# Who writes the waits: an agent attention and maxout FFN kernel whose semaphores are set by its own plan

## The chip, the cores and the metric

The kernel runs on one core of a Trainium2 chip. A core has five engines, each with its own instruction stream: PE (TensorE, matrix products), ACT (ScalarE), DVE (VectorE), POOL (GpSimd) and SP (SyncE, which here issues the transfers). They are kept in step by semaphores: an instruction may wait until a counter has reached a value, and may raise a counter when it is done. PE's products arrive in PSUM; everything else lies in SBUF. The metric is device time in microseconds (us); lower is better. The time before is 453.33 us, the median of three runs (451.63 to 454.15).

## The reference

Four batches of N = 12544 rows with C = 128 columns each, and 49 agents a batch. Agents first gather from keys and values, then each query gathers from the agents, and the result goes through a feed forward layer with three hidden branches of 768 columns:

```python
scale = 1.0 / np.sqrt(128)
a2k = softmax(scale * agents @ k.T)        # 49 x 12544
agent_v = a2k @ v                          # 49 x 128
q2a = softmax(scale * q @ agents.T)        # 12544 x 49
x = q2a @ agent_v                          # all batches: 50176 x 128
h = np.maximum(np.maximum(x @ w1, x @ w2), x @ w3)
out = h @ w_out
```

## The kernel before, in words

The kernel never forms x. For each batch it multiplies the 49 rows of agent values into the weights, w3 - w1, w2 - w1 and w1 @ w_out, and keeps the products in a tile G. A query's exponentials (49 values) times G then give the hidden layer directly. max(max(a, b), c) is computed as a plus two clipped differences, and the division by the softmax sum is done at the very end.

The work is cut into 49 groups s of 1024 rows (eight tiles of 128; the last group takes the last two tiles of each batch). For a group the steps are, with their names in the plan: `ql` loads the queries, `qc` casts them on POOL, `qt`/`qe` turn them on PE and copy them out on DVE (from s = 38 on a transposing transfer `qd` does it), `sc` and `ex` form scores and exponentials, `su` and `re` the reciprocal sums. Then for six blocks f of the hidden layer `u.s.f` (PE, line 558) and `a.s.f` (ACT, 571), `v.s.f` (PE, 558) and `x.s.f` (DVE, the max, 574); for f = 4 the clips are both on ACT (565 and 568) and `v` adds into the bank of `u`. Each hidden product is two matmuls on the two halves of the array's rows. `li` (582) and `p` (592) form the output in two halves o = 0, 1; `ov` (599) scales each half on DVE, and `st` (607) stores it.

Keys and values of batch 0 are worked first (steps `kl0`, `kc0`, `kt0`, `ke0`, `ks0`, `kx0`, `to0`, `vc0`, `kv0`); those of the next batches (`kl`, `kc`, `kt` as a transposing transfer, `ks`, `kx`, `kv`, `va`, `ea`, and at the end `fo`, `to`, `nr`, `gp`, `gv`) are hosted inside the query groups of the batch before.

The order of all steps, and the buffer that each new tile takes (the number after the slash), is written out by hand in the text `ORDER`: three two-bank PSUM buffers UV for hidden products, two PSUM banks OM for all else, thirteen load buffers LD and so on. Each engine executes its own steps in that order. What the text does not say is which instruction waits for which. In the kernel before this is found out by the framework that builds the program: a buffer is a tile of a pool with its number as tag, and every use of it is followed by the framework, which places waits and increments. Transfers share a small set of completion semaphores.

A step is a function of `Emit` that issues its instructions; `Plan.add` in `graph` states its engine, the steps that it follows (`after`), the tiles that it makes (`new`) and uses (`use`). The loop that runs them is:

```python
for name in order:
    o = plan.ops[plan.index[name]]
    for t in o["new"]:
        self.new(plan.tiles[t], t)
    o["fn"]()
```

Of the kernel before, what the change touches and what calls it, by code (L numbers as in the profile page):

```python
# [9 lines left out]
FP32 = mybir.dt.float32  # L10
BF16 = mybir.dt.bfloat16
# [16 lines left out]
PE, ACT, DVE, POOL, SP = range(5)  # L28
ROW, FULL, COL = range(3)
# [11 lines left out]
class Plan:  # L41
# [5 lines left out]
    def add(self, name, eng, fn, cost, mode=FULL, after=(), new=(), use=(), bank=None, serve=0.0):  # L47
        self.index[name] = len(self.ops)
        for cls, t in new:
# [4 lines left out]
                             new=[t for _, t in new], use=[t for _, t in new] + list(use), bank=bank, serve=serve))  # L54

    def places(self, order, given):
# [16 lines left out]
        return place  # L73

# [41 lines left out]
def graph(plan, em):  # L116
# [3 lines left out]
    add("prep", PE, em.prep, (0.3, 3.6))  # L120
# [21 lines left out]
    for g in range(SPARE):  # L142
        add(f"wm.{g}", PE, em.warm(g), (0.2225, 0.45), new=[("UV", f"warm.{g}")])
# [15 lines left out]
    add("rc0", DVE, em.recip_first, (0.85, 0.97), after=[f"to0.{g}" for g in range(last + 1)], new=[("KR", "kr0")], use=["acc"])  # L159
# [9 lines left out]
    add("el", ACT, em.evacuate_linear, (0.17, 0.31), after=["pl"], use=["pl"])  # L169
# [5 lines left out]
    for b in range(1, B):  # L175
        ch = chunks(b)
        for g, (t0, n) in enumerate(ch):
# [9 lines left out]
            add(f"ks{r}", PE, em.k_scores(b, g, n, m), mm(n, 49), after=[f"kt{r}"], new=[("OM", m)], use=[f"kT{r}"], bank=m)  # L187
# [72 lines left out]

class Emit:
    def __init__(self, nc, pools, io):
        self.nc, self.pools, self.io = nc, pools, io
        self.t, self.place = {}, {}
        nc_, const = nc, pools["const"]
        self.ident = const.tile([P, P], BF16, name="ident")
        make_identity(nc, self.ident)
        self.ones = const.tile([P, P], FP32, name="ones")
        nc.vector.memset(self.ones, 1.0)
        self.ones_bf = const.tile([P, P], BF16, name="ones_bf")  # L270
        nc.vector.memset(self.ones_bf, 1.0)
        self.avT = [const.tile([P, H], BF16, name=f"avT{i}") for i in range(2)]
        for t in self.avT:
            nc.vector.memset(t, 0.0)
        self.agT = const.tile([P, B, H], BF16, name="agT")
        nc.vector.memset(self.agT, 0.0)
        self.sel = const.tile([P, 2], BF16, name="sel")
        nc.vector.memset(self.sel, 0.0)
        nc.vector.memset(self.sel[:A, 0:1], 1.0)
        nc.vector.memset(self.sel[H:H + A, 1:2], 1.0)  # L280
        self.ag_st = const.tile([A, B, C], FP32, name="ag_st")
        nc.scalar.dma_start(self.ag_st, io["agents"].rearrange("b a c -> a b c"))
# [5 lines left out]
        nc.vector.memset(self.wall[:, C1O:], 0.0)  # L288
# [14 lines left out]
    def run(self, plan, order, given):  # L303
        self.place = plan.places(order, given)
        for name in order:
            o = plan.ops[plan.index[name]]
            for t in o["new"]:
                self.new(plan.tiles[t], t)
            o["fn"]()


    def prep(self):
        nc = self.nc
        nc.vector.tensor_copy(out=self.ag_bf, in_=self.ag_st)
        t = self.pools["psum"].tile([P, 512], FP32, tag="OM0", name="OM0").bitcast(BF16)
        for b in range(B):
            nc.tensor.transpose(t[:, b * H:b * H + A], self.ag_bf[:, b, :], self.ident[:A, :A])
        for b in range(B):
            nc.vector.tensor_copy(out=self.agT[:, b, :A], in_=t[:, b * H:b * H + A])
# [545 lines left out]
```

## Time and profile before

| what | value |
|---|---|
| median of three runs | 453.33 us (451.63 to 454.15) |
| profiled execution, first to last instruction (span) | 449.8 us |
| granted clock of PE | 0.996 |
| instructions | 13103 |
| PE, DVE, ACT busy | 94%, 90%, 88% of the span |
| POOL busy | 38% |
| DMA | 117.80 MB, mean 262 GB/s |

The profile gives of one execution the span alone; the time of a run is measured from outside and is some 3.5 us longer. In the profile's rows, PE is matmuls and PEld the loading of weights, which overlaps them; "TILE<-A,B" is the output and the inputs by the program's names; "[0.41 <-PE UV L558]" behind an instruction says that its engine was idle for 0.41 us before it, and that the product of line 558 into UV ended this. Instructions that only wait are not counted as busy.

### The profile page before, as it was taken

The numbers are of one execution on the slowest core, as the hardware profiler recorded it, in microseconds if no ns is written. First come the engines' busy times: TensorE is split into PE (matmuls) and PEld (weight loads), VectorE is DVE, ScalarE is ACT, GpSimd is POOL, SyncE is SP. The second block draws the span as 40 slices with busy tenths as digits, with TensorE's granted clock in tenths as the row PEclk, the third lists the DMA queues.
The fourth block names the chain that finished last, engine by engine and source line by source line (L and its number), as shares of the span: only waits on it lengthen the run. The fifth ranks groups of instructions, "written<-read, shape, count | busy, mean of one in ns | idle before, by whom it ended". The sixth has DMA issues, their size and how long they took to land.

```text
span 449.8 us, 13103 instructions
## 1 busy us (share of the span) xinstructions
PE 423.7 (94%) x5388; PEld 274.0 (61%) x5388; DVE 402.8 (90%) x512; ACT 395.1 (88%) x461; POOL 169.4 (38%) x176
## 2 busy tenths in 40 slices
PE   0778899999999999999999999999999999999996
PEld 0654466666665666666666666666666655565675
DVE  1335999999999999999999999999999999999986
ACT  1459999999988999999989999999889899999983
POOL 1641645455676372464363263453402110100000
PEclk9989999999999999999999999999999999999999
DMA  8999999999999998999969799498608685327142
GB/s 311 409 408 387 326 373 310 263 394 316 340 320 274 392 216 223 408 273 318 406 200 324 216 350 226 141 314 336 212 6 230 191 221 129 96 103 178 48 177 107
DMA packets 80150, 117.80 MB, mean 262 GB/s; under 512 B 53527, under 2 KB 56283, under 8 KB 80091
## 3 DMA queue, kind: packets, MB, share of 16 engines
q1 hardware_dynamic: 79888, 116.87, 83.6%
q8 instruction: 42, 0.69, 0.6%
q14 instruction: 17, 0.14, 0.1%
q10 hardware_dynamic: 203, 0.10, 0.1%
HBM read 78.74 MB, written 25.69 MB: 232 GB/s over the span
## 4 chain that ended last, share of the span: by engine, by line
PE 73%; DMA 12%; DVE 6%; POOL 2%; ACT 2%; SPq 2%; issue 2%; POOLq 0%; DVEq 0%
PE UV L558 29%; PE OM L592 27%; DMA LD<-in_k_dram 6%; PE OM L582 5%; DMA LD<-in_v_dram 4%; DVE R L574 4%; PE OM L523 3%; PE OM L533 3%; PE OM L376 2%; DMA out_dram<-OS 2%; PE OM L359 2%; DVE OS L599 1%; SPq L454 1%; ACT AS L571 1%; ACT VB L333 1%
## 5 line engine op out<-in xcount | busy, mean ns | idle before, releaser
L574 DVE TENSOR_TENSOR R<-UV,AS 128x1024 bf16<-128x1024 f32 x245 | 293.4, 1219 | 11.4 <-PE UV L558 5.3
L571 ACT ACTIVATE AS<-UV 128x1024 bf16<-128x1024 f32 x245 | 246.7, 1023 | 18.3 <-PE UV L558 11.7
L558 PE MATMUL UV<-EQ,G 49*128 49x512 bf16 (+1 forms) x1248 | 178.5, 368 | 2.1 <-DVE R L574 1.3
L592 PE MATMUL OM<-wo_bf,R 128*128 128x128 bf16 x2352 | 179.8, 219 | 0.0
L592 PEld LDWEIGHTS <-R 128*128 128x128 bf16 x2352 | 139.7, 98 | 39.5 <-issue 37.3
L558 PEld LDWEIGHTS <-G 49*128 49x128 bf16 x1248 | 58.7, 93 | 63.9 <-issue 23.8
L517 POOL CAST QB<-LD 128x1024 bf16<-128x1024 f32 x49 | 50.8, 1040 | 111.9 <-DMA LD<-in_q_dram 50.6
L599 DVE TENSOR_TENSOR OS<-OM,RC 128x512 f32<-128x512 f32 x98 | 67.3, 686 | 2.6 <-PE OM L592 1.4
L335 POOL CAST KB<-LD 128x1152 bf16<-128x1152 f32 (+2 forms) x45 | 49.7, 1116 | 40.6 <-DMA LD<-in_k_dram 35.9
L335 POOL CAST VB<-LD 128x1152 bf16<-128x1152 f32 (+1 forms) x33 | 37.3, 1137 | 40.4 <-DMA LD<-in_v_dram 24.3
L568 ACT ACTIVATE R<-UV 128x1024 bf16<-128x1024 f32 x49 | 50.1, 1022 | 2.5 <-PE UV L558 1.7
L565 ACT ACTIVATE UV<-UV 128x1024 f32<-128x1024 f32 x49 | 49.9, 1019 | 2.3 <-DVE R L574 1.2
L582 PE MATMUL OM<-G,EQ 128*128 128x256 bf16 x196 | 37.9, 275 | 0.0
L474 POOL TENSOR_TENSOR EA<-EA,EK 128x441 f32<-128x441 f32 x27 | 27.6, 1023 | 18.5 <-ACT EK L365 18.1
L539 ACT ACTIVATE EQ<-OM 128x512 bf16<-128x512 f32 x49 | 29.4, 601 | 1.0 <-PE OM L533 0.9
L527 DVE COPY QT<-OM 128x1024 bf16<-128x1024 bf16 x38 | 26.0, 684 | 1.1 <-PE OM L523 1.0
L347 DVE COPY KT<-UV 128x1152 bf16<-128x1152 bf16 (+1 forms) x12 | 8.2, 700 | 18.2 <-PE UV L342 18.2
L523 PE MATMUL OM<-ident,QB 128*128 128x128 bf16 x304 | 23.7, 222 | 0.6 <-POOL QB L517 0.6
L582 PEld LDWEIGHTS <-EQ 128*128 128x128 bf16 x196 | 12.3, 97 | 15.9 <-issue 15.2
L523 PEld LDWEIGHTS <-QB 128*128 128x128 bf16 x304 | 18.5, 99 | 4.3 <-issue 2.6
L359 PEld LDWEIGHTS <-KT 128*128 128x128 bf16 x392 | 14.3, 98 | 10.0 <-issue 5.5
L533 PE MATMUL OM<-QT,agT 128*64 128x512 bf16 (+1 forms) x104 | 20.2, 393 | 0.0
(67 smaller groups left out, 196.4 us busy)
## 6 DMA issues: line engine op xcount, KB each, us to landing
LD<-in_q_dram SPq DMA_DIRECT2D x48, 512.0 KB, 6.6
out_dram<-OS SPq DMA_DIRECT2D x48, 512.0 KB, 6.3
LD<-in_k_dram SPq DMA_DIRECT2D x40, 576.0 KB, 7.8
LD<-in_v_dram SPq DMA_DIRECT2D x40, 576.0 KB, 9.4
LD<-in_k_dram SPq DMA_DIRECT2D x3, 512.0 KB, 6.0
LD<-in_v_dram SPq DMA_DIRECT2D x3, 512.0 KB, 11.4
LD<-in_moe_w_dram SPq DMA_DIRECT2D x6, 192.0 KB, 8.4
KT<-KB SPq DMA_TRANSPOSE x33, 6.7
```

The source lines that it names most:

```text
L335: (self.nc.gpsimd if eng == POOL else self.nc.vector).tensor_copy(out=out, in_=src)
L517: return lambda: self.nc.gpsimd.tensor_copy(out=self.t[f"qb.{s}"], in_=self.t[f"q.{s}"][:, :GT, :])
L523: self.nc.tensor.transpose(t[:, j * P:(j + 1) * P], self.t[f"qb.{s}"][:, j, :], self.ident)
L533: self.nc.tensor.matmul(self.t[f"qs.{s}"][h * H:(h + 1) * H, jj * P:(jj + pairs) * P], self.agT[:, b, :], self.t[f"qT.{s}"][:, 2 * jj + h: ...
L558: self.nc.tensor.matmul(t[:, h, jj * P:(jj + pairs) * P], self.t[f"G{b}"][h * H:h * H + A, c + f * P:c + (f + 1) * P], self.t[f"e.{s}"][h ...
L565: return lambda: self.nc.scalar.activation(self.t[f"u.{s}.{f}"], self.t[f"u.{s}.{f}"], AF.Relu)
L568: return lambda: self.nc.scalar.activation(self.t[f"r.{s}.{f}"], self.t[f"u.{s}.{f}"], AF.Relu)
L571: return lambda: self.nc.scalar.activation(self.t[f"a.{s}.{f}"], self.t[f"u.{s}.{f}"], AF.Relu)
L574: return lambda: self.nc.vector.tensor_tensor(out=self.t[f"r.{s}.{f}"], in0=self.t[f"v.{s}.{f}"], in1=self.t[f"a.{s}.{f}"], op=ALU.max)
L582: self.nc.tensor.matmul(self.t[f"o.{s}.{o}"][:, i * 2 * C:(i + 1) * 2 * C], self.t[f"e.{s}"][:, jj * P:(jj + 1) * P], self.t[f"G{of[jj]}"] ...
L592: self.nc.tensor.matmul(self.t[f"o.{s}.{o}"][:, c:c + C], self.t[f"r.{s}.{f}"][:, h, jj * P:(jj + 1) * P], self.wo_bf[:, f, :], start=Fals ...
L599: self.nc.vector.tensor_tensor(out=self.t[f"os.{s}"][:, j:j + 4, :], in0=self.t[f"o.{s}.{o}"].rearrange("p (j c) -> p j c", c=C), in1=self ...
```

## The change

Order, buffers and arithmetic stay. The kernel no longer lets the framework find the waits. All buffers become fixed tiles, one for each place, and the new function `Plan.waits` walks the order once and works out for every step which earlier steps it has to wait for: those named in `after`, the makers of its tiles, the last users of a buffer that it takes over, and whoever else touched a PSUM bank. It keeps for each engine (and each destination of transfers) how far the others are known to have come, including what those had waited for themselves; what is already known is left out. Of steps of PE and of SP on their own engine nothing is waited for. `Emit.run` then issues the waits: all but the last as separate wait instructions in the engine's stream, the last one on the first instruction of the step. Only steps that somebody waits for raise a counter, with their last instruction; every transfer raises the counter of its destination buffer by 16. After the last step POOL waits for the final value of every counter. All of it stands in a critical section of the framework.

So that the plan knows everything, what was set up outside the order (identity, ones, agents) becomes steps of it; the preparation, the first reciprocal, the fold and the normalisation, whose instructions depend on one another, are split into one step for each, and a few steps name predecessors that they did not name before.

```diff
-    def add(self, name, eng, fn, cost, mode=FULL, after=(), new=(), use=(), bank=None, serve=0.0):
+    def add(self, name, eng, fn, cost, mode=FULL, after=(), new=(), use=(), bank=None, serve=0.0, dma=False):
         self.index[name] = len(self.ops)
         for cls, t in new:
             self.tiles[t] = cls
             self.maker[t] = name
         seq = [self.maker[t] for t in use if self.maker[t] not in after]
         self.ops.append(dict(name=name, eng=eng, fn=fn, pace=cost[0], lat=cost[1], mode=mode, after=list(after), seq=seq,
-                             new=[t for _, t in new], use=[t for _, t in new] + list(use), bank=bank, serve=serve))
+                             new=[t for _, t in new], use=[t for _, t in new] + list(use), bank=bank, serve=serve,
+                             dma=dma or eng == SP))
...
+    def waits(self, order, place):
+
+        known = {e: {} for e in range(5)}
+        snap, at, count = {}, {}, {}
+        users, slot_users, seen = {}, {}, {}
+        out, told = {}, set()
+        rank = {n: i for i, n in enumerate(order)}
+        for name in order:
+            o = self.ops[self.index[name]]
+            e = o["eng"]
+            need = set(o["after"])
+            for t in o["use"]:
+                cls = self.tiles[t]
+                key = (cls, place[t])
+                if t in o["new"]:
+                    slot_users[t] = users.get(key, {})
+                    users[key] = {}
+                m = self.maker[t]
+                if m != name and m not in need and (cls in PSUM or self.ops[self.index[m]]["eng"] == e):
+                    need.add(m)
+                elif t in o["new"] or m not in need:
+                    need.update(slot_users[t].values())
+                if cls in PSUM:
+                    need.update(x for k, x in users[key].items() if k != (e, False))
+            need.discard(name)
+            here = known[e]
+            todo = {}
+            for x in need:
+                p = self.ops[self.index[x]]
+                who, pos = at[x]
+                if who == e and (e == PE or e == SP):
+                    continue
+                if who not in todo or todo[who][0] < pos:
+                    todo[who] = (pos, x)
+            kept = []
+            for who, (pos, x) in sorted(todo.items(), key=lambda z: str(z[0])):
+                if here.get(who, -1) >= pos:
+                    continue
+                if any(w != who and snap[y].get(who, -1) >= pos for w, (_, y) in todo.items()):
+                    continue
+                kept.append(x)
+            for x in kept:
+                who, pos = at[x]
+                for w, v in list(snap[x].items()) + [(who, pos)]:
+                    if here.get(w, -1) < v:
+                        here[w] = v
+                told.add(x)
+            kept.sort(key=lambda x: rank[x])
+            out[name] = kept
+            who = e if not o["dma"] else (o["lane"] if "lane" in o else self.lane(o, place))
+            pos = count.get(who, 0)
+            count[who] = pos + 1
+            at[name] = (who, pos)
+            snap[name] = dict(here)
+            for t in o["use"]:
+                users[(self.tiles[t], place[t])][(e, o["dma"])] = name
+        return out, told, at
+
+    def lane(self, o, place):
+        t = o["new"][0] if o["new"] else o["use"][0] if o["use"] else None
+        return "AG" if t is None else f"{self.tiles[t]}{place[t]}"
...
-    add("prep", PE, em.prep, (0.3, 3.6))
+    add("id0", POOL, em.clear_ident, (0.3, 0.6))
+    add("id", POOL, em.make_ident, (0.3, 0.6), after=["id0"])
+    add("ones0", DVE, em.make_ones, (1.0, 1.1))
+    add("ones", DVE, em.make_sel, (0.15, 0.2), after=["ones0"])
+    add("agl", ACT, em.load_agents, (0.5, 5.0), dma=True)
+    add("agc", DVE, em.cast_agents, (0.42, 0.52), after=["agl"])
+    add("agt", PE, em.turn_agents, (0.2, 0.4), after=["agc", "id"], new=[("OM", "agt")])
+    add("prep", DVE, em.place_agents, (0.4, 0.5), after=["agt", "ones"], use=["agt"])
...
-    add("rc0", DVE, em.recip_first, (0.85, 0.97), after=[f"to0.{g}" for g in range(last + 1)], new=[("KR", "kr0")], use=["acc"])
+    add("rs0", DVE, em.reduce_first, (0.5, 0.6), after=[f"to0.{g}" for g in range(last + 1)], new=[("KR", "kr0")], use=["acc"])
+    add("rc0", DVE, em.recip_first, (0.35, 0.4), after=["rs0"], use=["kr0"])
...
-            add(f"ks{r}", PE, em.k_scores(b, g, n, m), mm(n, 49), after=[f"kt{r}"], new=[("OM", m)], use=[f"kT{r}"], bank=m)
+            add(f"ks{r}", PE, em.k_scores(b, g, n, m), mm(n, 49), after=[f"kt{r}", "prep"], new=[("OM", m)], use=[f"kT{r}"], bank=m)
...
-        add(f"fo{b}", POOL, em.fold(b), (1.25, 1.35), after=[f"ea{b}.{g - 1}"], new=[("ES", f"es{b}")], use=[f"ea{b}"])
+        for i in range(3):
+            add(f"fo{b}.{i}", POOL, em.fold(b, i), (0.33, 0.4), after=[f"fo{b}.{i - 1}" if i else f"ea{b}.{g - 1}"], use=[f"ea{b}"])
+        add(f"fo{b}", POOL, em.fold(b, 3), (0.25, 0.3), after=[f"fo{b}.2"], new=[("ES", f"es{b}")], use=[f"ea{b}"])
...
-        add(f"nr{b}", DVE, em.normalise(b, m), (0.5, 0.62), after=[f"to{b}", f"va{r}"], new=[("KR", f"kr{b}"), ("G", f"G{b}")],
-            use=[m, f"va{b}"], bank=m)
+        held = [f"gp{x}" for x in "abcd"] + ["gl"] if b == 2 else [f"gp{x}{b - 2}" for x in "acl"] if b > 2 else []
+        add(f"kr{b}", DVE, em.reciprocal_of(b, m), (0.25, 0.3), after=[f"to{b}"], new=[("KR", f"kr{b}")], use=[m], bank=m)
+        add(f"nr{b}", DVE, em.normalise(b, m), (0.25, 0.32), after=[f"kr{b}", f"va{r}"] + held, new=[("G", f"G{b}")],
+            use=[f"kr{b}", f"va{b}"])
...
-            add(f"gp{name}{b}", PE, em.product(b, c0, c1, f"gp{name}{b}"), mm(1, w), mode=COL, after=[f"nr{b}", "el"],
+            add(f"gp{name}{b}", PE, em.product(b, c0, c1, f"gp{name}{b}"), mm(1, w), mode=COL, after=[f"nr{b}", "el", "d31a", "d31b", "d32", "d21a", "d21b"],
...
+class Recorder:
+
+
+    def __init__(self, engine, made):
+        self.engine, self.made = engine, made
+
+    def __getattr__(self, name):
+        call = getattr(self.engine, name)
+
+        def record(*args, **named):
+            i = call(*args, **named)
+            self.made.append(i)
+            return i
+        return record
+
+
+class Engines:
+    def __init__(self, nc):
+        self.made = []
+        for n in ("tensor", "vector", "scalar", "gpsimd", "sync"):
+            setattr(self, n, Recorder(getattr(nc, n), self.made))
...
-    def new(self, cls, name):
-        shape, dt = SHAPE[cls]
-        tag = f"{cls}{self.place[name]}"
-        t = self.t[name] = self.pools["psum" if cls in ("UV", "OM") else "sbuf"].tile(shape, dt, tag=tag, name=tag)
-        return t
+        for cls, n in SLOTS.items():
+            shape, dt = SHAPE[cls]
+            for i in range(n):
+                self.slots[cls, i] = pools["psum" if cls in PSUM else "sbuf"].tile(shape, dt, name=f"{cls}{i}")
+
+    def run(self, plan, order, place, tc):
+
+        made = self.nc.made
+        for t, i in place.items():
+            self.t[t] = self.slots[plan.tiles[t], i]
+        waits, told, at = plan.waits(order, place)
+        sems, count, mark, final = {}, {}, {}, {}
+        for name in order:
+            o = plan.ops[plan.index[name]]
+            for x in waits[name][:-1]:
+                who, value = mark[x]
+                self.queues[o["eng"]].wait_ge(sems[who], value)
+            made.clear()
+            o["fn"]()
+            for x in waits[name][-1:]:
+                who, value = mark[x]
+                made[0].wait_op(sems[who], value, "sem-ge")
+            if o["dma"] or name in told:
+                who = at[name][0]
+                if who not in sems:
+                    sems[who] = tc.alloc_semaphore(f"s{who}")
+                for i in made if o["dma"] else made[-1:]:
+                    step = 16 if o["dma"] else 1
+                    i.then_inc(sems[who], step)
+                    count[who] = count.get(who, 0) + step
+                mark[name] = (who, count[who])
+                final.pop(who, None)
+                final[who] = count[who]
+        for who, value in final.items():
+            self.queues[POOL].wait_ge(sems[who], value)
...
-    with tc.manual_schedule():
-        em.run(plan, order, given)
+    place = plan.places(order, given)
+    with tc.tile_critical():
+        em.run(plan, order, place, tc)
```

More of the change, by code (lines that the diff above doesn't have):

```diff
@@ L168, in graph @@
     add("pl", PE, em.prep_linear, mm(NF, 128), after=["ew1", "cwo"], new=[("OM", "pl")])
-    add("el", ACT, em.evacuate_linear, (0.17, 0.31), after=["pl"], use=["pl"])
+    add("el", ACT, em.evacuate_linear, (0.17, 0.31), after=["pl", "ones"], use=["pl"])
     add("gl", PE, em.product(0, C1O, WC, "gl"), mm(1, 256), mode=COL, after=["nr0", "el"], new=[("OM", "gl")])
@@ L301, in half, with cast_agents, turn_agents, place_agents @@
         return t.bitcast(BF16)
[L303 to L315, printed above, removed]
+    def cast_agents(self):
+        self.nc.vector.tensor_copy(out=self.ag_bf, in_=self.ag_st)
+    def turn_agents(self):
+        t = self.half("agt")
         for b in range(B):
-            nc.tensor.transpose(t[:, b * H:b * H + A], self.ag_bf[:, b, :], self.ident[:A, :A])
+            self.nc.tensor.transpose(t[:, b * H:b * H + A], self.ag_bf[:, b, :], self.ident[:A, :A])
+    def place_agents(self):
         for b in range(B):
-            nc.vector.tensor_copy(out=self.agT[:, b, :A], in_=t[:, b * H:b * H + A])
+            self.nc.vector.tensor_copy(out=self.agT[:, b, :A], in_=self.half("agt")[:, b * H:b * H + A])
     def kv_load(self, which, b, t0, n):
```

66 lines of the change are left out of this document (36 added, 30 removed).

## The prediction

> **What bounds the kernel now.** I read the page first: the busy shares, the chain that ended last, then the groups.
>
> ```profile
> span 449.8 us, 13103 instructions
> PE 423.7 (94%) x5388; PEld 274.0 (61%) x5388; DVE 402.8 (90%) x512; ACT 395.1 (88%) x461; POOL 169.4 (38%) x176
> PE 73%; DMA 12%; DVE 6%; POOL 2%; ACT 2%; SPq 2%; issue 2%; POOLq 0%; DVEq 0%
> ...
> L574 DVE TENSOR_TENSOR R<-UV,AS 128x1024 bf16<-128x1024 f32 x245 | 293.4, 1219 | 11.4 <-PE UV L558 5.3
> L571 ACT ACTIVATE AS<-UV 128x1024 bf16<-128x1024 f32 x245 | 246.7, 1023 | 18.3 <-PE UV L558 11.7
> ```
>
> Three engines are near full and each hands to the next, so a share does not say which one decides; the chain is 73% on PE. A busy PE is not PE at its peak, so I looked at how often matmuls really start. This is PE's timeline: start, length, line, count.
>
> ```profile
> 285.10 0.38 PE L592 MATMUL OM<-wo_bf,R 128*128 128x128 bf16 x4
> 285.41 0.82 PE L558 MATMUL UV<-EQ,G 49*128 49x512 bf16 x6
> 286.17 0.39 PE L582 MATMUL OM<-G,EQ 128*128 128x256 bf16 x2
> 286.39 0.39 PE L592 MATMUL OM<-wo_bf,R 128*128 128x128 bf16 x4
> 286.62 0.61 PE L523 MATMUL OM<-ident,QB 128*128 128x128 bf16 x8
> 287.06 0.39 PE L592 MATMUL OM<-wo_bf,R 128*128 128x128 bf16 x4
> 287.38 0.89 PE L558 MATMUL UV<-EQ,G 49*128 49x512 bf16 x6
> 288.21 1.01 PE L592 MATMUL OM<-wo_bf,R 128*128 128x128 bf16 x15
> ```
>
> Eight L523 take 287.06 - 286.62 = 0.44 us, 55 ns each; two L582 take 0.22, 110 ns each; the four L592 at 286.39 take 0.23 to the next start, 57 ns each. Six L558 are three products (two halves of the array side by side): 0.76 and 0.83 us. Three products at 0.215 are 0.645, and about 0.1 us is left whenever PE turns between full and split matmuls: the four L592 at 285.10 take 0.31 up to L558, 0.22 of it matmuls. So PE does in a quiet stretch what these prices say:
>
> ```profile
> 260.00:300.00 40.00, 40.00 (x531) 26.37 (x529) 39.07 (x50) 38.31 (x45) 20.91 (x20) 1.00 0.88 240
> ...
> 60.00:430.00 370.00, 367.48 (x4602) 233.91 (x4600) 357.77 (x437) 347.02 (x401) 144.76 (x147) 1.00 0.85 253
> ```
>
> (stretch, length, then busy time and count of PE, PEld, DVE, ACT, POOL, the granted clock, DMA share, GB/s). Over 60 to 430 us PE's groups are:
>
> ```profile
> L592 PE MATMUL OM<-wo_bf,R 128*128 128x128 bf16 x2156 | 165.6, 219 | 0.0
> L558 PE MATMUL UV<-EQ,G 49*128 49x512 bf16 x1084 | 164.1, 381 | 1.8 <-DVE R L574 1.3
> L582 PE MATMUL OM<-G,EQ 128*128 128x256 bf16 x182 | 35.2, 275 | 0.0
> L523 PE MATMUL OM<-ident,QB 128*128 128x128 bf16 x272 | 20.8, 219 | 0.0
> ```
>
> 2156 x 56 ns + 542 x 215 + 182 x 108 + 272 x 56 = 121 + 117 + 20 + 15 = 273 us; the small groups (L533, L359, L376, L545, the products of G) add about 31, and some 540 turns at 0.094, counted in the same timeline, add 51. That is 355 of 370 us. So the steady stage is PE's own work to within about 14 us, and only those 14 can be had from quicker waits. The clock is 1.00, so none of it is the clock. DVE needs 39.07 and ACT 38.31 of 40: close behind, and it is their lateness that makes PE wait.
>
> The first 40 us have another bound, transfers (DMA share 0.97), and SP's DMA issues there stop behind earlier transfers:
>
> ```profile
> 0.00:40.00 40.00, 22.48 (x320) 16.99 (x320) 12.69 (x33) 18.66 (x27) 14.09 (x19) 0.96 0.97 379
> ```
>
> **The change part by part.** It moves no arithmetic. Removed are wait instructions and waits; added are some wait instructions, and the place of a wait on its instruction changes.
>
> (1) *Waits that sat on an instruction of their own.* Before, 5388 + 5388 + 512 + 461 + 176 instructions are counted as work, 11925 of 13103; with 246 DMA issues about 930 are left that only wait or signal. Their price shows where an engine starts straight behind a product. Start of the product on PE against start of its reader:
>
> ```profile
> 237.10 0.60 PE L558 MATMUL UV<-EQ,G 49*128 49x512 bf16 x4
> ...
> 233.47 0.60 PE L558 MATMUL UV<-EQ,G 49*128 49x512 bf16 x4
> ...
> 427.99 0.39 PE L558 MATMUL UV<-EQ,G 49*128 49x512 bf16 x2
> ```
> ```profile
> 237.60 1.23 DVE L574 TENSOR_TENSOR R<-UV,AS 128x1024 bf16<-128x1024 f32 x1 [0.41 <-PE UV L558]
> ...
> 428.42 2.39 DVE L574 TENSOR_TENSOR R<-UV,AS 128x1024 bf16<-128x1024 f32 x2 [0.23 <-PE UV L558]
> ```
> ```profile
> 233.90 1.02 ACT L571 ACTIVATE AS<-UV 128x1024 bf16<-128x1024 f32 x1 [0.63 <-PE UV L558]
> ```
>
> At 237.10 the reader comes 0.50 us behind, at 233.47 and 427.99 0.43. DVE's max has two makers (PE and ACT), ACT's first relu one; the same max comes at either distance, so it is not the engine, and I take 65 ns as the price of a wait that ends on an instruction of its own, and the change puts the latest wait on the working instruction. It counts only where the reader is already waiting:
>
> ```profile
> ACT AS L571 <- PE UV L558: 11.7, 38, 0.8
> ...
> DVE R L574 <- PE UV L558: 5.3, 17, 0.6
> ...
> PE UV L558 <- DVE R L574: 1.3, 3, 0.8
> ```
>
> (total us, times, longest). 55 such waits at 65 ns are 3.6 us of reader time, but PE loses only where its bank is then late. Of some 96 places where PE starts right behind a releaser, 43 have a releaser that was itself late by such an instruction: 43 x 65 ns = 2.8, and about half of it is made up again before PE needs it. I take -2.5 (1.5 direct, the rest because each delay also makes later ones); ends: 0, and -14, all of PE's waiting; -5 is as far as I call plausible.
>
> (2) *Where PE's wait sits.* Before, a hidden product's wait for its bank stands on the matmul and its weights are loaded ahead. After, the wait is put on the first instruction of the step, and if that becomes the weight load, the load starts only when the bank is free:
>
> ```profile
> L558 PEld LDWEIGHTS <-G 49*128 49x128 bf16 x1248 | 58.7, 93 | 63.9 <-issue 23.8
> ```
>
> In the places where load and matmul begin together already, the reader came 0.43 instead of 0.42 behind, so the real price is about 14 ns: the matmul follows into the part of the array that is loaded. With some 92 waits that bind and 60 close to it, 150 x 14 ns = 2.1 at most; I take +1.0. If instead each costs the whole 93 ns it is 150 x 93 = +14, of which about +11 stays, since some fall into idle turns.
>
> The Trainium skill ("TensorE: Matmul & The Clock Gate", Step-by-step: what each phase is for) says that PE's queue reorders only weight loads, ahead of matmuls in flight; by that rule a load that carries a wait can no longer run ahead, and its section LDWEIGHTS (loading the stationary operand) would price it, as an estimate, at 128/1.2 = 107 ns, +16 us here. The trace has 93 ns for the same load, and no row of before shows a load held by a bank.
>
> (3) *Wait instructions on PE.* 130 to 150 steps of PE keep two waits (K scores: transfer and slot; values: ACT and POOL; turns: POOL and slot), so PE gets about as many new instructions. Behind each stand the products of the next tiles, and DVE and ACT wait for those. Most run under PE's queue; some 5 bind, 5 x 65 ns = +0.3 (0 to 140 x 65 ns = 9).
>
> (4) *Semaphores per destination.* Shared ones make a DMA issue wait for an unrelated transfer, in the start above all: loads go out about 1.5 us apart there.
>
> ```profile
> 11.35 0.33 SPq L391 DMA_DIRECT2D LD<-in_moe_w_dram  x1
> 12.85 0.33 SPq L325 DMA_DIRECT2D LD<-in_v_dram  x1
> ```
>
> But the DMA share is 0.97, so an earlier issue only queues: -0.3 (0 to -1). Cover gone, i.e. engines not full, each such wait would be worth about a microsecond.
>
> (5) *Entry and end.* The whole plan runs in a critical section with an own final wait of POOL for every counter. Nothing in the trace shows such a section; the nearest rows are the opening up to the first load and the last:
>
> ```profile
> 0.74 0.87 SPq L325 DMA_DIRECT2D LD<-in_k_dram  x2
> ```
>
> The setup, one barrier among it, takes 0.74: I take +0.2 at entry (0 to 0.74) and +0.3 at the end (0 to 0.74).
>
> (6) *The last store.* Before, the first of st.48's four transfers leaves when half the output is scaled:
>
> ```profile
> 445.65 1.79 SPq L607 DMA_DIRECT2D out_dram<-OS  x4
> ```
> ```profile
> 444.93 1.36 DVE L599 TENSOR_TENSOR OS<-OM,RC 128x512 f32<-128x512 f32 x2 [0.59 <-PE OM L592]
> ```
>
> After, the step waits for both halves: 444.93 + 1.36 = 446.29 instead of 445.65, and the four issues stand one behind the other: +0.6.
>
> The split preparation, fold and normalisation (0 each) issue the same instructions in the same order; POOL, with 20.91 busy of 40, hides the fold, and DVE's stall for the normalisation was there.
>
> Sum: -2.5 + 1.0 + 0.3 - 0.3 + 0.2 + 0.3 + 0.6 = -0.4 us on a span of 449.8. Median before 453.33, 3.5 us above that span (451.63 to 454.15); the parts outside the span do not change, so 453.33 - 0.4 = 452.9 us.
>
> **The rivals.** *Quicker handovers propagate.* PE, DVE and ACT form one loop, and a delay in each comes back as a later bank. For it: three engines at 38 to 40 of 40 us and 14 us of PE's waiting. Against: in the quiet stretch hardly anything is waited for. If half the waiting goes: -7 + 1.9 = -5, 448 us.
>
> *Weight loads are held by their waits* (ends on the other side). Place: the first matmul of each hidden product; price 93 ns; it decides once more than 30 of the 150 are exposed (30 x 93 = 2.8, more than part 1 gives). For it: the wait goes on the first instruction of a step. Against: the 14 ns seen where both start together. +11 - 2.5 + 0.4 = +9, 462 us.
>
> *The critical section costs a real barrier at both ends* and waits on PE bind more often: +1.5 at entry and end, +2 on PE: 456 us.
>
> *It prunes what never bound*: the waits that decide are the ones kept, everything of part 1 is 0: 453.33 + 2.1 = 455.4, no change that can be told.
>
> **How the numbers follow.** About 0.5%, 2.3 us, is what a measurement of this kernel can tell from no change. Forecast as summed: 0.38, its own range 450.5 to 455; propagation 0.34, spread over 446 to 451; loads held 0.11; section 0.09; pruned for nothing 0.08. Faster takes propagation and a little of the forecast's lower end: 0.38. Slower takes loads, section and a little of the upper end: 0.21. Same: 0.41. The range leaves out the worst of the loads case and the far end of propagation: 446 to 458.5.
>
> **What would show it.** Part 1: DVE's max starts 0.43 instead of 0.50 behind its product, and the idle time before L574 and L571 falls from 11.4 and 18.3. Part 2: L558's weight loads start together with their matmuls, and the distance to the next product tells 14 or 93 ns. Part 3: PE's turns to L359, L376 and L523 lengthen. Part 4: the loads at 11 to 20 us leave closer together without landing earlier. Part 6: the last store leaves at the end of the second L599. Wrong would be a PE whose waits beyond 60 us shrink by half (faster than forecast), or turns that grow above 0.1 us (slower).

## The result, and the profile after

The changed kernel takes 455.97 us (median of 12 runs, 453.88 to 458.6) against 452.33 (median of 12, 451.18 to 454.71) of the kernel before: ratio 1.0077, 95% interval 1.0054 to 1.010. It is slower by 0.8%, some 3.5 us. The forecast was 452.9 and no change; the range, 446 to 458.5, holds the time, but slower had only 0.21.

All instructions now carry one line, L347, because one recording function issues them; read them by their tiles. The page after, in the order of the page before:

```profile
span 454.3 us, 12617 instructions
PE 424.4 (93%) x5388; PEld 264.3 (58%) x5388; DVE 402.6 (89%) x512; ACT 395.2 (87%) x461; POOL 169.8 (37%) x176
PE 72%; DMA 14%; SPq 4%; ACT 3%; DVE 3%; POOL 2%; issue 1%; DVEq 0%
...
L347 DVE TENSOR_TENSOR R<-UV,AS 128x1024 bf16<-128x1024 f32 x245 | 292.8, 1218 | 9.4 <-PE UV L347 6.0
L347 ACT ACTIVATE AS<-UV 128x1024 bf16<-128x1024 f32 x245 | 246.8, 1023 | 20.2 <-PE UV L347 14.6
```

486 instructions are gone, and the work of each engine is the same. What is new is in the chain: SP's queue has 4% of it, 2% before. So I looked at where the 4.5 us of span arise, first by the scalings of the output (each 1024 rows end with one). Tile OS on DVE in two windows, 55 to 67 and 440 to 456 us; the times are those of the first and of the last start. Before:

```profile
L599 DVE TENSOR_TENSOR OS<-OM,RC x3: 680/692/694, 55.1 to 63.1; 128x512 f32<-128x512 f32 x3
...
L599 DVE TENSOR_TENSOR OS<-OM,RC x4: 681/688/692, 440.7 to 445.6; 128x512 f32<-128x512 f32 x4
```

After:

```profile
L347 DVE TENSOR_TENSOR OS<-OM,RC x2: 680/686/691, 60.1 to 64.2; 128x512 f32<-128x512 f32 x2
...
L347 DVE TENSOR_TENSOR OS<-OM,RC x5: 636/679/691, 439.4 to 449.1; 128x512 f32<-128x512 f32 x5
```

The first scaling comes 60.1 - 55.1 = 5.0 us late, the last 449.1 - 445.6 = 3.5. The loss is there before the first output; over the 48 groups behind it the changed kernel wins 1.5 us back. The rest of the span is the end: from the last scaling's start to the last instruction it is 454.3 - 449.1 = 5.2 us instead of 449.8 - 445.6 = 4.2. Together 5.0 - 1.5 + 1.0 = 4.5, the difference of the spans.

Now the start. Stretches of 3 us (length, PE, PEld, DVE, ACT, POOL, granted clock, DMA share, GB/s), before:

```profile
36.00:39.00 3.00, 2.17 (x21) 1.03 (x20) 0.66 (x2) 3.00 (x6) 0.00 (x0) 1.00 1.07 385
39.00:42.00 3.00, 2.50 (x36) 1.39 (x37) 2.11 (x7) 2.51 (x4) 0.00 (x0) 1.00 1.03 387
45.00:48.00 3.00, 2.00 (x19) 0.87 (x16) 2.92 (x3) 2.57 (x5) 2.79 (x3) 1.00 1.00 397
```

After:

```profile
36.00:39.00 3.00, 2.15 (x32) 1.14 (x30) 1.07 (x3) 3.00 (x6) 0.00 (x0) 1.00 0.43 159
39.00:42.00 3.00, 1.86 (x26) 0.73 (x22) 1.54 (x6) 1.52 (x3) 0.00 (x0) 1.00 0.67 192
45.00:48.00 3.00, 1.80 (x12) 0.88 (x10) 0.97 (x3) 1.99 (x3) 1.04 (x1) 0.50 1.01 362
```

From 36 to 42 us the transfers, which bound this stage, move less than half as much (159 and 192 GB/s instead of 385 and 387). Later PE's clock is at half. SP's timeline and its waits say why the transfers stop. After:

```profile
25.49 14.47 SPq L347 DMA_DIRECT2D LD<-in_moe_w_dram  x5
40.07 0.37 SPq L347 DMA_DIRECT2D LD<-in_q_dram  x1
40.48 0.43 SPq L347 DMA_DIRECT2D LD<-in_k_dram  x1
40.96 0.43 SPq L347 DMA_DIRECT2D LD<-in_moe_w_out_dram  x1
```
```profile
SPq L347 <- DMA LD<-in_moe_w_dram: 9.6, 1, 9.6
```

Before:

```profile
28.85 5.30 SPq L391 DMA_DIRECT2D LD<-in_moe_w_dram  x5
35.31 0.33 SPq L513 DMA_DIRECT2D LD<-in_q_dram  x1
36.72 0.33 SPq L325 DMA_DIRECT2D LD<-in_k_dram  x1
38.21 0.39 SPq L389 DMA_DIRECT2D LD<-in_moe_w_out_dram  x1
```

Five weight loads go out in 5.3 us before and in 14.5 after, with one wait of 9.6 us for a weight load. The three hidden weights are loaded in two halves each into one buffer (`lw1a` and `lw1b`, and so on). `Plan.waits` sees that `lw1b` uses the tile that `lw1a` made, on the same engine, and takes `lw1a` as needed; and since a transfer is on the list of its destination and not of SP, the rule that SP does not wait for itself does not spare it. So the second half waits until the first has landed, behind all that SP had put into the queue earlier, and everything behind it on SP waits too: the other two second halves, queries, keys of the next batch, w_out. The two halves write different columns; the wait protects nothing but the count, since both raise one counter.

### The profile page after: what moved, and what is told of

It reads as the page before. It is cut to its first block, busy times and chain, and to the rows that moved or that the text cites. A ratio compares the mean times of both kernels' runs of the same rounds, so it can differ in the third digit from the quotient of the medians.

```text
span 454.3 us, 12617 instructions
## 1 busy us (share of the span) xinstructions
PE 424.4 (93%) x5388; PEld 264.3 (58%) x5388; DVE 402.6 (89%) x512; ACT 395.2 (87%) x461; POOL 169.8 (37%) x176
## 4 chain that ended last, share of the span: by engine, by line
PE 72%; DMA 14%; SPq 4%; ACT 3%; DVE 3%; POOL 2%; issue 1%; DVEq 0%
PE OM L347 43%; PE UV L347 29%; DMA LD<-in_v_dram 6%; SPq L347 4%; DMA LD<-in_q_dram 3%; DMA KT<-KB 2%; DMA out_dram<-OS 2%; DMA LD<-in_moe_w_out_dram 2%; DVE R L347 2%; ACT AS L347 1%; ACT VB L347 1%; DVE OS L347 1%; POOL QB L347 1%; POOL KB L347 0%; POOL EA L347 0%
## 5 line engine op out<-in xcount | busy, mean ns | idle before, releaser
L347 DVE TENSOR_TENSOR R<-UV,AS 128x1024 bf16<-128x1024 f32 x245 | 292.8, 1218 | 9.4 <-PE UV L347 6.0
L347 ACT ACTIVATE AS<-UV 128x1024 bf16<-128x1024 f32 x245 | 246.8, 1023 | 20.2 <-PE UV L347 14.6
L347 PE MATMUL OM<-wo_bf,R 128*128 128x128 bf16 x2352 | 179.8, 219 | 0.0
L347 PE MATMUL UV<-EQ,G 49*128 49x512 bf16 (+1 forms) x1248 | 178.9, 372 | 0.6
L347 PEld LDWEIGHTS OM<-wo_bf,R 128*128 128x128 bf16 x2352 | 139.7, 98 | 39.6 <-issue 37.5
L347 POOL CAST QB<-LD 128x1024 bf16<-128x1024 f32 x49 | 50.9, 1042 | 109.3 <-DMA LD<-in_q_dram 60.6
L347 PEld LDWEIGHTS UV<-EQ,G 49*128 49x128 bf16 x1248 | 49.5, 93 | 71.4 <-ACT AS L347 16.9
L347 DVE TENSOR_TENSOR OS<-OM,RC 128x512 f32<-128x512 f32 x98 | 67.3, 687 | 4.5 <-PE OM L347 2.0
L347 POOL CAST KB<-LD 128x1152 bf16<-128x1152 f32 (+2 forms) x45 | 49.8, 1118 | 41.1 <-DMA LD<-in_k_dram 40.0
L347 POOL CAST VB<-LD 128x1152 bf16<-128x1152 f32 (+1 forms) x33 | 37.4, 1139 | 45.7 <-PE OM L347 29.5
L347 ACT ACTIVATE UV<-UV 128x1024 f32<-128x1024 f32 x49 | 49.9, 1019 | 3.9 <-PE UV L347 3.6
L347 ACT ACTIVATE R<-UV 128x1024 bf16<-128x1024 f32 x49 | 50.1, 1022 | 1.9 <-PE UV L347 1.5
L347 PE MATMUL OM<-G,EQ 128*128 128x256 bf16 x196 | 38.0, 275 | 0.0
L347 POOL TENSOR_TENSOR EA<-EA,EK 128x441 f32<-128x441 f32 x27 | 27.7, 1026 | 19.5 <-ACT EK L347 19.1
L347 ACT ACTIVATE EQ<-OM 128x512 bf16<-128x512 f32 x49 | 29.5, 601 | 1.3 <-PE OM L347 1.2
L347 DVE COPY QT<-OM 128x1024 bf16<-128x1024 bf16 x38 | 26.0, 684 | 3.3 <-PE OM L347 3.3
L347 PE MATMUL OM<-ident,QB 128*128 128x128 bf16 x304 | 24.5, 227 | 1.8 <-POOL QB L347 1.2
L347 DVE COPY KT<-UV 128x1152 bf16<-128x1152 bf16 (+1 forms) x12 | 8.2, 698 | 17.8 <-PE UV L347 17.8
L347 PEld LDWEIGHTS OM<-ident,QB 128*128 128x128 bf16 x304 | 19.1, 101 | 5.9 <-issue 2.7
L347 PEld LDWEIGHTS OM<-G,EQ 128*128 128x128 bf16 x196 | 12.1, 97 | 15.8 <-issue 7.8
L347 PE MATMUL OM<-QT,agT 128*64 128x512 bf16 (+1 forms) x104 | 20.6, 403 | 0.0
L347 ACT ACTIVATE EK<-OM 128x441 bf16<-128x441 f32 (+1 forms) x33 | 17.8, 539 | 1.5 <-PE OM L347 1.0
```

Of the source, the lines that this page charges most:

```text
L347: i = call(*args, **named)
```

## The experiments

**The wait alone, taken out and put in.** In the changed kernel each second half gets a counter of its own and no longer waits for the first:

```diff
         add(f"l{w}b", SP, em.w_load(w, DFF // 2, DFF), use=[w], **dma(196))
+        plan.ops[-1]["lane"] = f"{w}b"
...
                 m = self.maker[t]
-                if m != name and m not in need and (...):
+                if "lane" in o:
+                    need.update(slot_users[t].values())
+                elif m != name and m not in need and (...):
```

> The changed kernel, but the second half of each hidden weight no longer waits for the first half's transfer to land; each second half raises a counter of its own. Theory (the loss is that wait: SP stops, everything behind it on SP comes late): the DMA share between 36 and 45 us is back at about 1.0 (0.43 and 0.67 in the changed kernel), PE's granted clock stays at 1.0 after 45 us, the first group's output ends near 60 us instead of 64.9, and the time is 451 to 452 us, a little under the kernel before. Rival one (the start is late by its split preparation and its clock): the first output stays beyond 63.5 us and the time at 455 to 456. Rival two (the loss lies in the steady stage, where PE's waits sit on weight loads): the time stays above 454 too, and the lag grows group by group.

Measured: 452.04 us, ratio to the kernel before 0.9994 (0.9975 to 1.0012). Scalings, weight loads and one stretch of this kernel:

```profile
L350 DVE TENSOR_TENSOR OS<-OM,RC x3: 681/691/692, 55.0 to 63.0; 128x512 f32<-128x512 f32 x3
```
```profile
25.74 4.51 SPq L350 DMA_DIRECT2D LD<-in_moe_w_dram  x5
```
```profile
36.00:39.00 3.00, 2.28 (x23) 1.04 (x20) 0.60 (x1) 3.00 (x7) 0.00 (x0) 1.00 1.06 383
```

The loads go out in 4.5 us, the share is 1.06, the first scaling is at 55.0: the loss at the first output is gone with this one wait. The time is just at the upper end of the expected 451 to 452. This kernel's last scaling starts at 444.9 us. Against it the changed kernel is 60.1 - 55.0 = 5.1 us late at the first scaling and 449.1 - 444.9 = 4.2 at the last, so 0.9 of the 1.5 us above is, by these two traces, lateness that is made up on the way, and only 0.6 is won by the kernel with free halves too.

Then the kernel before, with nothing but that wait; its framework sets it when the halves overlap by one column:

```diff
-        add(f"l{w}b", SP, em.w_load(w, DFF // 2, DFF), use=[w], **dma(196))
+        add(f"l{w}b", SP, em.w_load(w, DFF // 2 - 1, DFF), use=[w], **dma(196))
```

> The kernel before with that wait alone: the second half of each hidden weight is loaded from one column earlier, so that the two halves overlap by a column (same values) and the framework makes the second wait for the first. Theory: 4 to 5 us slower than before, 456 to 457.5 us, with a hole in the DMA share after 36 us and a granted clock under 1.0 after 45 us. Rivals: within 1 us of the kernel before.

Measured: 457.65 us, ratio 1.0114 (1.0074 to 1.0154), a little above the expected 456 to 457.5. These are four runs that lie far apart, 454.78 to 459.96, and the profiled one is the fastest of them. The same hole appears in it:

```profile
28.64 11.10 SPq L391 DMA_DIRECT2D LD<-in_moe_w_dram  x5
```
```profile
36.00:39.00 3.00, 2.18 (x21) 1.04 (x21) 0.67 (x2) 3.00 (x6) 0.00 (x0) 1.00 0.43 161
39.00:42.00 3.00, 1.44 (x28) 0.83 (x28) 0.97 (x2) 1.83 (x2) 0.00 (x0) 1.00 0.69 208
...
L599 DVE TENSOR_TENSOR OS<-OM,RC x3: 682/691/691, 58.2 to 66.2; 128x512 f32<-128x512 f32 x3
```

The wait stands 6.9 us here instead of 9.6, the granted clock falls to 0.60 from 45 to 48 us, and the first scaling is 58.2 - 55.1 = 3.1 us late instead of 5.0.

Taken out of the one kernel and put into the other, the wait moves the time by -0.8% and +1.1%. That shows the cause from both sides; rivals one (the split preparation) and two (the steady stage) fall.

**Is the clock a part of it?** PE's clock of 0.5 after 45 us could have been the larger half of the damage. Idle matmuls were put into PE's holes in the changed kernel, first into one, then into all three:

```diff
     def warm(self, g):
-        return lambda: self.nc.tensor.matmul(self.t[f"warm.{g}"][:, 0, :], ...)
+        def fn():
+            for _ in range(10 if g == SPARE - 1 else 1):
+                self.nc.tensor.matmul(self.t[f"warm.{g}"][:, 0, :], ...)
+        return fn
...
- gvd cwo qt.1/0
+ gvd cwo wm.8/0 qt.1/0
...
- u.0.4/2 pl/1
+ u.0.4/2 wm.9/1 pl/1
```

(wm.8 and wm.9, eight matmuls each, are in the second run only.)

> The changed kernel, its weight halves still waiting, and ten idle matmuls instead of one in the hole before the product of the second weight halves (from 40.8 us on), so that PE does not fall idle there. It tells the clock's part of the loss from the late data's. If PE's clock of 0.5 from 45 to 54 us comes from that hole and costs what the first output lost beyond the late transfers (5.0 - 3.8 = 1.2 us): the clock stays at 1.0, the first output ends near 63.7, the time is about 1 us lower, 455. If the late data are all of it: the time stays at 456 whatever the clock.

> The changed kernel, its weight halves still waiting, with idle matmuls in all three holes that PE has between 41 and 50 us: ten ahead of the product of the second weight halves, eight each ahead of the turn of the second query group and of the product of w1 with w_out. In the run before, with the first hole alone filled, the clock fell later, from 51 to 58 us, instead. If the clock's fall is part of the loss: with all holes filled the clock stays at 1.0, the first output ends 1 us or more earlier than 64.9 and the time is 455 us or less. If the late data are all of it: the first output at 64 to 65 and the time at 456, although the clock stays.

Measured: 456.27 us, ratio 1.0093 (1.0068 to 1.0119), and 455.99, ratio 1.0060 (1.0038 to 1.0083), where the changed kernel has 1.0077. With one hole filled the clock fell later (to 0.57 and 0.50 from 51 to 57 us), with all three it stayed up. Stretches and scalings of the second:

```profile
45.00:48.00 3.00, 2.63 (x16) 1.07 (x15) 1.87 (x4) 2.56 (x3) 0.34 (x1) 1.00 1.07 378
48.00:51.00 3.00, 3.00 (x23) 1.41 (x22) 1.82 (x2) 1.01 (x1) 2.48 (x3) 1.00 1.04 412
```
```profile
L349 DVE TENSOR_TENSOR OS<-OM,RC x2: 680/686/691, 59.8 to 63.9; 128x512 f32<-128x512 f32 x2
```

The clock is 1.00 instead of 0.50, and the first scaling still starts at 59.8 instead of 60.1. So the clock alone does not make the loss. How much of it is the clock's stays open, for two reasons. The ratios 1.0060 and 1.0077 differ by 0.17%, and by the widths of their intervals up to about 0.5%, some 2 us, may lie between them. And the idle matmuls fill PE themselves (3.00 of 3.00 us from 48 to 51), so they may cost what the clock gives.

One trace hints that such a fall is not free at the first output. The kernel with the split last store and the one with the loads written out on top of that (both below) have no wait between the halves, and the transfers of the second leave no later (w_out at 36.40 us against 36.89). In its profiled run the clock happened to be at 0.5 from 46.5 to 53.4 us, in that of the first not. A stretch and the first scalings of the first, then of the second:

```profile
48.00:51.00 3.00, 2.69 (x24) 0.91 (x21) 2.50 (x3) 2.66 (x5) 0.81 (x2) 1.00 1.27 148
...
L355 DVE TENSOR_TENSOR OS<-OM,RC x3: 680/692/692, 55.0 to 63.4; 128x512 f32<-128x512 f32 x3
```
```profile
48.00:51.00 3.00, 3.00 (x20) 1.10 (x19) 1.86 (x2) 2.29 (x3) 1.46 (x2) 0.50 1.31 196
...
L359 DVE TENSOR_TENSOR OS<-OM,RC x3: 680/691/693, 56.7 to 64.7; 128x512 f32<-128x512 f32 x3
```

PE is full at half its clock, and the first scaling comes 1.7 us late; the last starts at 444.2 us in both, so all of it is made up on the way. The fall was not made on purpose, so this is a hint and no test. Another hint: of the four runs of the kernel before with the wait, the fastest has the highest mean clock (454.78 us, 0.992) and the slowest the lowest (459.96, 0.976).

**The last store.** In addition to the free halves, the last store becomes four steps, the first two waiting for the first half of the output alone:

```diff
+        if s == NQ - 1:
+            for r in range(B):
+                add(f"st.{s}.{r}", SP, em.store_row(s, r), after=[f"ov.{s}.{r // 2}"], use=[f"os.{s}"], ...)
+                plan.ops[-1]["lane"] = f"st{r}"
+            continue
```

> As the first, and the last store in four steps, the first two of which wait for the first half of the output alone. Theory (the last store's wait sets the end): its first transfer leaves about 0.65 us earlier against the end of the last scaling, and the time is 0.6 us under the first kernel of this call. Rival (the last transfer sets the end, whenever the first leaves): less than 0.2 us.

Measured: 450.56 us, ratio 0.9968 (0.9952 to 0.9984): faster than both kernels. The last transfers of the changed kernel, then of this one:

```profile
449.78 1.80 SPq L347 DMA_DIRECT2D out_dram<-OS  x4
```
```profile
444.10 1.80 SPq L355 DMA_DIRECT2D out_dram<-OS  x4
...
L355 DVE TENSOR_TENSOR OS<-OM,RC x3: 681/692/692, 440.8 to 444.2; 128x512 f32<-128x512 f32 x3
```

The last scaling starts at 449.1 and 444.2 us, so the store begins 0.7 us behind that start in the one and 0.1 us ahead of it in the other. From the last scaling's start to the end of the span it is 450.2 - 444.9 = 5.3 us with the free halves alone (its last scaling starts at 444.9), and 448.7 - 444.2 = 4.5 here: 0.8 us for the split. The medians differ by 1.5 us; the other 0.7 lies between the groups, where nothing was changed, and is within what two sets of 12 runs differ by.

**Weight loads.** On top of that, the loads of the hidden products are written out and the wait for the bank stands on the matmul behind them, as in the kernel before:

```diff
-                    self.nc.tensor.matmul(t[...], G..., e..., start=..., stop=True, ...)
+                    load = pe.add_instruction(mybir.InstLdweights(..., ins=[G...], tile_size=(H, P), tile_position=(row, 0)))
+                    mul = pe.add_instruction(mybir.InstMatmult(..., ldweights=False))
...
-                made[0].wait_op(sems[who], value, "sem-ge")
+                made[1 if name in plan.late else 0].wait_op(sems[who], value, "sem-ge")
```

> As the third, and the weight loads of the hidden products are instructions of their own, with the wait for the bank on the matmul behind them, as in the kernel before. By the trace's 14 ns for each held load, of which some 170 bind: 0.5 to 2 us under the third kernel. If a held load cost its whole 93 ns: 8 us or more under it. If nothing hangs on it: within 0.3 us of it.

Measured: 450.70 us, ratio 0.9971 (0.9955 to 0.9987), the same as without, to within about 1 us. The changed kernel and this one have the same place in the order; here is the group of three products in it, PE and its loads, in the changed kernel:

```profile
345.82 1.17 PE L347 MATMUL UV<-EQ,G 49*128 49x512 bf16 x6
346.92 0.40 PE L347 MATMUL OM<-wo_bf,R 128*128 128x128 bf16 x4
```
```profile
346.59 0.10 PEld L347 LDWEIGHTS UV<-EQ,G 49*128 49x128 bf16 x2 [0.41 <-DVE R L347]
```

and with the waits on the matmuls:

```profile
341.11 1.16 PE L759 MATMUL UV<-EQ,G 49*128 49x512 bf16 x6
342.20 0.40 PE L359 MATMUL OM<-wo_bf,R 128*128 128x128 bf16 x4
```

In the first, the load waits 0.41 us for DVE and starts only then; yet from the first of the three products to the next line it is 346.92 - 345.82 = 1.10 us, against 342.20 - 341.11 = 1.09. Over all such places from 60 us on, a matmul starts 58 ns behind its releaser with the load held and 55 to 56 with it free (some 220 places each).

**The order of two waits, and the pruning.** Basis is the kernel with free halves and split store, 450.56 us. First the wait that is latest in the order is made the instruction of its own; then nothing is pruned:

```diff
-            kept.sort(key=lambda x: rank[x])
+            kept.sort(key=lambda x: -rank[x])
```
```diff
-                if here.get(who, -1) >= pos:
-                    continue
-                if any(w != who and snap[y].get(who, -1) >= pos for w, (_, y) in todo.items()):
-                    continue
```

> The kernel with free weight halves and the split last store, but where a step has several waits the order is turned round: the latest wait is the instruction of its own, the earliest stands on the working instruction. The number of waits is the same. Theory (a wait that ends on an instruction of its own costs its reader 65 ns): DVE's max starts 0.50 us behind its product wherever it has two waits, and the time is 0.5 to 1.5 us above the same kernel with the order as it was (450.6). Rival (handover does not reach the end, because PE's own work sets it): within 0.4 us.

> The same kernel as the basis of the first, with nothing pruned: every step waits for the last step of each engine that it needs, known or not: 1248 wait instructions on PE instead of 76, 389 on ACT instead of 97, 493 on DVE instead of 107. Theory (waits that are already fulfilled run under the work of a full engine, except on PE, where those that bind are few): 1 to 4 us slower, nearly all from PE. Rival one (each instruction on PE's queue costs 65 ns in the open): 1172 x 0.065 = 76 us slower. Rival two (pruning is worth nothing): within 0.4 us.

Measured: 452.39 us, ratio 1.0006 (0.9982 to 1.0030), and 453.40, ratio 1.0025 (1.0003 to 1.0048), both against the kernel before; the basis has 0.9968 (0.9952 to 0.9984). So the order of two waits is worth 0.4%, 1.7 us, a little over what was expected, and the pruning 0.6%, 2.6 us; the intervals leave more than 1 us on either side of both. A place in the first, PE and ACT:

```profile
199.86 0.60 PE L355 MATMUL UV<-EQ,G 49*128 49x512 bf16 x4
```
```profile
200.35 1.02 ACT L355 ACTIVATE AS<-UV 128x1024 bf16<-128x1024 f32 x1 [0.20 <-PE UV L355]
```

0.49 us behind the product. Counted over 66 to 430 us, where ACT or DVE waited over 60 ns for a product and its start can be told:

| kernel | ACT at 0.42 to 0.44 | ACT at 0.48 to 0.50 | DVE at 0.42 to 0.44 | DVE at 0.48 to 0.51 |
|---|---|---|---|---|
| before | 62 | 20 | 14 | 29 |
| changed | 78 | 0 | 40 | 0 |
| latest wait on its own | 50 | 36 | 34 | 5 |
| nothing pruned | 78 | 2 | 38 | 0 |

There are two distances and nothing between. That nothing pruned costs 2.6 us without touching them says that its price is elsewhere: in 1172 more wait instructions on PE (1248 instead of 76), 292 more on ACT, 386 on DVE, 164 on SP and 65 on POOL. No run tells these apart. If all of it were PE's, it would be about 2 ns for each, not the 65 of an instruction that ends a wait.

**Once more the clock.** The basis, with four idle matmuls instead of one at three places of the start:

```diff
-        return lambda: self.nc.tensor.matmul(self.t[f"warm.{g}"][:, 0, :], ...)
+            for _ in range(4 if g in (0, 1, SPARE - 1) else 1):
+                self.nc.tensor.matmul(self.t[f"warm.{g}"][:, 0, :], ...)
```

> The kernel with free weight halves and the split last store, with four idle matmuls instead of one at three places of the start, where PE waits for transfers and its clock falls to 0.6 for some microseconds. If that clock costs anything, 0.3 to 1 us faster than without them (450.6). If transfers set the start: the same within 0.3 us, whatever the clock shows.

Measured: 450.43 us, ratio 0.9961 (0.9940 to 0.9981). The mean clock in the profiled run is 1.000, against 0.995 of the basis, and the times can't be told apart. The fall that this removes lies at 30 to 36 us (0.63 and 0.80 in the basis), where the DMA share is 1.01 to 1.03: there transfers set the pace. It and its basis are among the best kernels of this study.

## Why the prediction was wrong

The step that failed is part 4, "Semaphores per destination". It counted only what a counter of one's own takes away, waits for unrelated transfers, and put -0.3 us (0 to -1) on it, with no end on the slower side. It did not ask which transfers share a destination. Two halves of a weight do, so the same edit adds three waits to SP's queue; one of them stands 9.6 us, and the term is +5.0 us at the first output. The diff shows it: the rule that makes a step wait for the maker of a tile that it uses names the engine, and then SP's own transfers are not spared, because `who` is their destination. The prediction costed what is queued behind a wait on PE and never did it for SP, though it wrote that "engines not full, each such wait would be worth about a microsecond". The share of 0.97 was taken as cover; it was cover for an earlier issue, not for a later one. What the part did count came as forecast: with free halves the five weight loads leave 3 us earlier than before (25.74 and 28.85 us), and the first scaling starts at 55.0 instead of 55.1.

That the range held 455.97 us is luck. Near it stood the rival of the critical section, 456 us, with +1.5 at entry and end and +2 on PE; what was measured at entry and end is +0.2 and +0.4 (part 5), and the time came from elsewhere. The rival that nothing of part 1 counts (455.4 us) falls too, since turning the order of two waits round costs 1.7 us.

*Part 1* was right in its mechanism; its size is smaller than forecast, as far as the runs tell it. 0.50 fell to 0.43 in every place that can be told (49 places at 65 ns, 3.2 us of reader time), and turning the order round costs 1.7 us. Predicted were -2.5 us. Parts 1 to 3 together were to give -1.2 between the first and the last scaling; the kernel with free halves won 0.6 there. The sign that was named for it, DVE's idle time ahead of its max, from 66 to 430 us before and after:

```profile
L574 DVE TENSOR_TENSOR R<-UV,AS 128x1024 bf16<-128x1024 f32 x225 | 269.3, 1218 | 9.9 <-PE UV L558 4.0 <-issue 0.5 <-PE OM L592 0.4
```
```profile
L347 DVE TENSOR_TENSOR R<-UV,AS 128x1024 bf16<-128x1024 f32 x225 | 268.9, 1218 | 6.6 <-PE UV L347 3.3 <-ACT AS L347 0.3
```

It fell by a third. ACT's over the same stretch did not (16.5 and 17.0 us): what DVE gains, ACT may wait again for PE, which does its own work; no run tests that. Propagation, the rival at 448 us, fell too: it needed half of PE's 14 us of waiting, and 0.6 us was won.

*Part 2*: the waits do sit on the loads now, as feared, but the price is 3 ns a place, not 14, and the times of the two kernels do not show it. The rival at 462 us falls: a matmul follows its load at once. The Trainium skill ("TensorE: Matmul & The Clock Gate", Architectural detail: the array is 16× 32×32, not 1× 128×128) states that a matmul can begin before its weight load has ended, part of the array computing while the rest still loads. The trace agrees: the matmul starts 58 ns behind its releaser, though the load ahead of it is recorded with 93 ns. The estimate of +16 us that the prediction drew from the same page's price of a load does not come true: that price is near the load's recorded length, and the matmul does not wait for all of it.

*Part 3*: PE has 76 wait instructions instead of 6, so 70 new ones and not 130 to 150; by the 2 ns of the unpruned kernel, an estimate at the upper side, they are 0.15 us, against +0.3; how many of them bind at 65 ns was not counted.

*Part 5*: SP's first load leaves at 0.96 instead of 0.74 us, +0.22 against +0.2; from the last store's first issue to the end of the span it is 454.3 - 449.78 = 4.5 us instead of 449.8 - 445.65 = 4.15, +0.37 against +0.3. Outside the span the prediction had taken 3.5 us, the median less the span of another run; a run's own time is 2.2 us above its span before (454.38 and 452.2 in one run) and 1.8 after (456.11 and 454.3 in the profiled run), so 0.4 of this comes back there. Nothing had suggested that.

*Part 6*: +0.6 predicted; the last store begins 449.78 - 449.1 = 0.7 us behind the last scaling's start, where it had begun together with it (445.65 and 445.6). Splitting the store again won 0.8 us from the last scaling to the end.

Had part 4 read +5.0, the sum would have been -0.4 + 5.3 = +4.9 on the span, where 4.5 was measured. That the two come so near is partly luck: 0.9 us of the late start was made up on the way, which no part had, and parts 1 to 3 won less than their sum.

## What to carry to other kernels

When waits are derived from tiles, list the transfers that write one tile in pieces: a pruner that knows tiles and not columns makes the second piece wait for the first, and on an in-order queue that wait holds up all transfers behind it. A full DMA share made an earlier issue worth nothing here, and did not cover a queue that stood for 9.6 us: for each new wait on an issuing queue, write down what stands behind it. Of two waits on a step, put the one that ends last on the working instruction; on a step whose engine already waits, it was worth 65 ns here.

## What the runs showed of the hardware

A wait that ends on an instruction of its own costs its reader 65 ns (0.50 instead of 0.43 us behind the product, in 49 places). Of waits that the plan knows to be fulfilled, 1172 more on PE and some 900 on the other engines cost 2.6 us together: about 2 ns for each of PE's if all of it were theirs. A weight load that is held by a wait delays its matmul by 3 ns (58 instead of 55 to 56 behind the releaser), though the load itself is recorded with 93 ns. The granted clock fell to 0.5 from 45 to 55 us in the changed kernel, where PE was short of data; with idle matmuls it stayed at 1.00, the first scaling came 0.3 us earlier and the time was the same within about 2 us. In one trace with the data on time, a fall from 46.5 to 53.4 us went with a first scaling 1.7 us late, and none of this was left at the last.
